# Weight tiles of the second matrix pair used from the buffer in which they are converted, transfers priced by their landing, bucket codes as float32r products

## The chip, the cores and the metric

One core of a Trainium2 chip runs the whole program. The metric is the device time of one execution in microseconds (us); less is better. The core has five engines: TensorE (PE; its weight loads are listed as PEld), VectorE (DVE), ScalarE (ACT), GpSimd (POOL) and SyncE (SP). Each has its own queue of instructions in a fixed order. Sixteen DMA engines move data between DRAM and SBUF. Nearly all transfers are issued from SyncE's queue.

## The reference

The program computes attention in which a query sees the keys of its own hash bucket only, and then two feed-forward blocks.

```python
# q, k, v: (2, 8, 768, 64) float32; proj: (64, 6)
q_bits = (einsum('bhsd,dk->bhsk', q, proj) > 0)
k_bits = (einsum('bhsd,dk->bhsk', k, proj) > 0)
q_bucket = sum(q_bits * 2**arange(6))
k_bucket = sum(k_bits * 2**arange(6))
scores = 0.125 * q @ k.T                       # per head
scores = where(q_bucket == k_bucket, scores, -1e9)
attn = softmax(scores)
x = (attn @ v) -> (1536, 512)
# block 1: w_in (512, 2048), w_out (2048, 512)
x = (s * relu(x @ w_in)**2 + b) @ w_out
# block 2: its own w_in, w_out
h = x @ w_in
out = (h * clip(h + 3, 0, 6) / 6) @ w_out      # (1536, 512)
```

The weight inputs are handed to the kernel as 64-bit words, two 32-bit words for each weight, and the kernel makes float32 of them on the chip.

## The kernel before

**Work.** The 1536 tokens are four units of 384 tokens. Attention runs over 16 pairs (a unit and two heads), and each pair has six slots (one head, 128 queries): 96 slots. A slot is a chain over engines: scores in float32r (`qk`, L417), row maximum (`smax`, L423, VectorE), exponent (`sexp`, L433, ScalarE), six transposes (`turn`, L439), eviction (`evict`, L452 or L454). After six slots come the products with V (`pv_mm`, L494). Before a pair's slots its keys and queries are loaded, split into a high and a low float32r part, and given bucket columns: the product with the projection (`bits_mm`, L379), the comparison with 0 (`bits`, L386), the product with a code matrix of +1 and -1 (`code_mm`, L393), and the comparison with the number of ones (`buckets`). The keys of the first four pairs are stored to DRAM (`k_store`, L327) and fetched again for the next unit (`k_fetch`, L330).

**Jobs.** The feed-forward part is eight jobs (`JOBS`, L30), each one block m for one unit j: (0,0), (0,1), (1,0), (1,1), (0,2), (0,3), (1,2), (1,3). A job goes through 32 weight tiles of 128 x 512: 16 of `w_in`, 16 of `w_out`. Each tile gives 12 matmuls of 128 x 128 by 384 columns (`mm`, L582): high part times high and low input, low part times high input. The numbers in `JOBS` (24, 16, 16, 16, 0 ...) say how many slots of attention of later units are due beside each job.

**Weight tiles.** A raw tile of 512 KB is loaded (`w_load`, L518) into one of three `wr` buffers. `w_exp` (L526, ScalarE) shifts the exponent. `w_ends` extracts two 16-bit halves into a `wf` buffer: the first on any of three engines (L538 on GpSimd, L540 on ScalarE), the second on VectorE (L535). `w_join` (L544, VectorE) joins them to float32. `w_store` (L550) writes the 256 KB to DRAM. For use, a tile is in a `wf` buffer (there are four): `w_hi` (L559, ScalarE) makes the high part in one of three `wh` buffers, `w_lo` (L565, GpSimd) the low part in one of three `wl` buffers. Job 0 uses its tiles from the `wf` buffer in which they were converted ("direct"). Every other job fetches them from DRAM (`w_fetch`, L554). The second pair of matrices is first used in job 2; in the kernel before it is converted ahead of that, stored, and then fetched by job 2 as by any other. Lines 740 to 758 hold this:

```python
direct = m == 0 and i < DIRECT                 # DIRECT = 32, so all of m == 0
ck = key if direct else ("c", m, i)
tw = t - 4.0 if direct else t - 12.0
add("DMA", tw - 4.0, (0.45, 1.46), w_load, (m, i, ck), needs=[("k", 1)] if m == 0 else [("mm", 1, 0)], ...
```

**The order.** Nothing is scheduled by hand: class `Plan` (L35) holds every step with its engine or engines, its duration, its due time, what it needs and gives, and the buffers that it takes and frees. `forward` is a list scheduler with a small model of the engines and of the DMA queue; `backward` turns a plan into latest start times, which are the due times of the next pass. `order` (L72) makes six passes and keeps the plan with the shortest modelled span. The steps are then issued in that order, so each engine's queue has a fixed order, and a step whose buffer or input is late holds all that stands behind it on its engine. A buffer is free when all the steps in its release list are done: a direct tile's `wf` when both the store and `w_lo` are.

**The first stage.** Unit 0's attention runs alone, with more score and raw buffers. Its tiles and buffers then give way to the 16 `G` tiles (the inner activations) and the `X` tiles (`later_units`, L289), which need the PV products and the key stores of the first four pairs.

Of the kernel before, what the change touches and what calls it, by code (L numbers as in the profile page):

```python
# [34 lines left out]
class Plan:  # L35
# [5 lines left out]
    PASSES, PREFER, BOOST = 6, 0, 30  # L41
    SAFE, LAT, DMA_LAT, SAME = 0.5, 0.2, 0.7, {"DVE": 0.1, "ACT": 0.1, "POOL": 0.1}

    WEIGHT = {"DVE": 1.0, "ACT": 0.7}
    EPS = {"PE": 0, "ACT": 0.15, "DVE": 0.3, "POOL": 0.15, "SP": 0.3}
# [26 lines left out]
    def order(self):  # L72

        due, best = [o[1] for o in self.ops], None
        for _ in range(self.PASSES):
            plan = self.forward(due)
            if best is None or plan[0] < best[0]:
                best = plan
            due = [min(x, o[9]) for x, o in zip(self.backward(*plan[:5]), self.ops)]
        self.span, self.log, self.where = best[0], best[5], best[6]  # L80
        return best[4]
# [45 lines left out]
    def forward(self, due):  # L127
# [13 lines left out]
        while left:  # L141
            able = {}
            for o in ready:
# [9 lines left out]
                else:  # L153
                    pick = None
                    for eng, dur in o[0].items():
                        wait = fits
                        for k in o[5]:
                            end, of = self.done[k]
                            wait = max(wait, end + (self.LAT if of != eng else self.SAME.get(eng, 0.0)))
                        if eng == "DMA":  # L160
                            wait = max(wait, clock["HW"], lanes[-8])
                            t, on = max(clock["SP"], wait), "SP"
                            if max(clock["ACT"], wait + self.SAFE) + self.PREFER < t:
                                t, on = max(clock["ACT"], wait + self.SAFE), "ACT"
# [4 lines left out]
                        end += self.WEIGHT.get(eng, 0.0) * (0 if eng == "DMA" else dur)  # L169
                        if pick is None or end < pick[0]:  # L170
                            pick = end, t, on, eng
# [26 lines left out]
            if eng == "DMA":  # L198
                clock["HW"] = t + dur[0]
                start = max(t + dur[0] + self.DMA_LAT, clock["DMA"])  # L200
                clock["DMA"] = end = start + dur[1]
                clock[on] = t + 0.1 if on == "ACT" else t + dur[0]
                lanes.append(end + self.LAT)
                of = "DMA queue"
            elif eng == "PE":
                clock[eng] = end = self.array(t, dur, 0.3 if fn.__name__ == "bits_mm" else 1.0)
                of = eng
            else:
                clock[eng] = end = t + dur
                of = eng  # L210
# [18 lines left out]
def attn_moe_moe2(ctx, tc, qT, kT, vN, cst, w1_in, w1_out, w2_in, w2_out, out):  # L229
# [35 lines left out]

    cv = const.tile([128, 420], F32, name="cv")
# [116 lines left out]
    def bits(g, nm):  # L383
        n = 128 if nm == "k" else 64
        t = at_p.tile([128, 384], F16, tag="bt", name="bt")
        nc.vector.tensor_scalar(out=t[0:n], in0=pd[g][nm + "h"][0:n, 0:384], scalar1=0.0, scalar2=None, op0=ALU.is_gt)  # L386
        pd[g][nm + "b"] = t

    def code_mm(g, nm, h):
        n = 128 if nm == "k" else 64  # L390
# [281 lines left out]
    for g in range(NP):  # L672
        u, hp = pairs[g]
        t = A[SPP * g] - 12.0
        own = new_keys(g)
        old = [g - 1] if 4 < g < 9 else [g - 2, g - 1] if g > 8 else [0] if g == 4 else []
        kfree = [("qk", SPP * x + i) for x in old for i in range(SPP)] + ([("ks", 0, 0), ("ks", 0, 1)] if g == 4 else [])
# [3 lines left out]
        if fetched:  # L681
            for x in range(2):
                add("DMA", t, (0.62, 2.2), k_fetch, (g, x), needs=kfree + [("ks", g - 4, 0), ("ks", g - 4, 1)], gives=[("kh", "kl")[x:x + 1] + (g,)])
        elif own:
            add("DMA", t, (0.62, 2.2), load_k, (g,), acq=[(("kr", "krx") if g < 4 else "kr", ("kr", g))], gives=[("k", g)])
            add({"ACT": 1.5, "POOL": 4.1, "DVE": 1.3}, t, 0, k_hi, (g,), needs=kfree + [("k", g)], gives=[("kh", g)], rel=[(("kr", g), 3)])
            add({"POOL": 3.7, "DVE": 2.0}, t, 0, k_lo, (g,), needs=[("kh", g)], gives=[("kl", g)], rel=[(("kr", g), 3)])
            if g < 4:
                for x in range(2):
                    add("DMA", t + 20.0, (0.62, 2.2), k_store, (g, x), needs=[("kl", g), ("kB", g), ("kB", g, 0)] if x else [("kh", g)], gives=[("ks", g, x)])  # L690
        add("DMA", t, (0.62, 1.1), load_q, (g,), acq=[(("qr", "qrx") if g < 4 else "qr", ("qr", g))], gives=[("q", g)])
        add({"ACT": 0.84, "POOL": 2.6, "DVE": 0.7}, t, 0, q_hi, (g,), needs=qfree + [("q", g)], gives=[("qh", g)], rel=[(("qr", g), 4)])
        add({"ACT": 0.84, "POOL": 2.4, "DVE": 0.7}, t, 0, q_top, (g,), needs=qfree + [("q", g)], gives=[("qt", g)], rel=[(("qr", g), 4)])
        add({"POOL": 4.0, "DVE": 1.22}, t, 0, q_lo, (g,), needs=[("qh", g)], gives=[("ql", g)], rel=[(("qr", g), 4)])
        for nm in ("kq" if own and not fetched else "q"):
            nh = 2 if nm == "k" else 1
            key = ("h", nm, g)
            add("PE", t, 0.85, bits_mm, (g, nm), needs=(kfree if nm == "k" else qfree) + [(nm, g)], acq=[(St, key)],
                gives=[(nm + "m", g)], rel=[((nm + "r", g), 3 if nm == "k" else 4)])
            add("DVE", t, 0.56, bits, (g, nm), needs=[(nm + "m", g)], acq=[("bt", ("bt", nm, g))], gives=[(nm + "b", g)])  # L700
            for h in range(nh):
                last = h == nh - 1
                add("PE", t, 0.5, code_mm, (g, nm, h), needs=[(nm + "b", g)] + ([(nm + "B", g, 0), "cd"] if h else ["cd"]),
                    gives=[(nm + "c", g, h)], rel=[(("bt", nm, g),)] if last else [])
                add({"DVE": 1.02} if nm == "q" else {"ACT": 0.85, "DVE": 1.02}, t, 0, buckets, (g, nm, h), needs=[(nm + "c", g, h)], gives=[(nm + "B", g, h), (nm + "B", g)] if last else [(nm + "B", g, h)],
                    rel=[(key,)] if last else [])
# [27 lines left out]
    for jn, (m, j, n) in enumerate(JOBS):  # L734
        t0, dt = M[jn]
        prev = [("mm", jn - 1, 28 + f // 4) if jn else None for f in range(16)]
        for i in range(32):
            key = (jn, i)
            t = t0 + i * dt
            if jn == first[m]:  # L740
                direct = m == 0 and i < DIRECT
                ck = key if direct else ("c", m, i)
                tw = t - 4.0 if direct else t - 12.0
                add("DMA", tw - 4.0, (0.45, 1.46), w_load, (m, i, ck), needs=[("k", 1)] if m == 0 else [("mm", 1, 0)],
                    acq=[("wr", ("wr", ck))], gives=[("wr",) + ck])
# [5 lines left out]
                last = [(("wf", ck), 1 + direct)]  # L751
                add("DMA", tw, (0.45, 0.73), w_store, (m, i, ck), needs=[("wf",) + ck], gives=[("ws", m, i)], rel=last)
            if jn != first[m] or not direct:
                add("DMA", t - 4.0, (0.45, 0.73), w_fetch, (m, i, key), needs=[("ws", m, i)] + past(jn, i, AHEAD) + before("wi", jn, i),
                    acq=[("wf", ("wf", key))], gives=[("wf",) + key, ("wi",) + key])
# [22 lines left out]
            elif i % 4 == 3:  # L778
# [73 lines left out]
```

## Time and profile before

| | |
|---|---|
| median of 3 runs | 870.61 us (866.76 to 871.86) |
| profiled execution | 870.84 us, its span 868.7 us |
| TensorE busy (PE), weight loads | 819.5 us (94%), 714.3 us (82%) |
| VectorE, ScalarE, GpSimd busy | 453.8, 533.9, 450.0 us |
| mean granted TensorE clock | 0.969 of full |
| DMA moved | 144.72 MB |
| transfers | 64 raw weight loads, 64 stores and 224 fetches of weight tiles |

The page cuts the span in 40 slices and gives every engine's busy share in each. TensorE's slices are at 7 to 9 tenths up to 360 us and at 9 from there, and its clock is at 8 or 9 tenths in the first two slices and between about 220 and 360 us. A busy TensorE is not one at its peak, since its matmuls are pipelined and their ends are modelled; for a stage the count of matmuls beside its length says more than the busy share.

### The profile page before, as it was taken

What the parts mean: (1) busy time and instruction counts of PE and PEld (TensorE: products, weight loads), DVE (VectorE), ACT (ScalarE), POOL (GpSimd) and SP (SyncE); (2) the same over time, 40 slices, a digit from 0 to 9 for tenths busy, and PEclk for the clock granted to TensorE, in tenths of its full rate; (3) what the DMA queues carried; (4) which work ended last, traced back from release to release, by engine and by line L of the source; (5) the groups of instructions that cost most, each with busy time, mean ns of one, the idle gap of its engine ahead of it and who ended that gap; (6) DMA issues with size and microseconds to landing.
All of it is one profiled execution on the core that took longest, in us unless ns stands there. A gap on an engine that the chain in (4) does not pass through costs nothing.

```text
span 868.7 us, 13213 instructions
## 1 busy us (share of the span) xinstructions
PE 819.5 (94%) x4668; PEld 714.3 (82%) x4668; DVE 453.8 (52%) x649; ACT 533.9 (61%) x965; POOL 450.0 (52%) x341
## 2 busy tenths in 40 slices
PE   7898899999887798899999999999999999999998
PEld 2555678879676776888787988889998999999998
DVE  6986489889485657574243656215423511510520
ACT  5766578868465655677474767547564744744742
POOL 4631076778463564653343445336544665665664
PEclk8899999999998879999999999999999999999999
DMA  9954077887577898643433323234433443444442
GB/s 354 396 186 146 19 237 233 226 292 231 175 243 241 283 316 254 215 125 107 119 109 112 103 92 112 88 98 126 118 90 86 123 132 121 125 140 149 124 140 75
DMA packets 63313, 144.72 MB, mean 167 GB/s; under 512 B 6800, under 2 KB 13072, under 8 KB 63248
## 3 DMA queue, kind: packets, MB, share of 16 engines
q1 hardware_dynamic: 63104, 143.68, 51.5%
q8 instruction: 36, 0.59, 0.3%
q14 instruction: 29, 0.24, 0.1%
q10 hardware_dynamic: 144, 0.22, 0.1%
HBM read 117.66 MB, written 26.21 MB: 166 GB/s over the span
## 4 chain that ended last, share of the span: by engine, by line
PE 73%; DMA 11%; DVE 7%; ACT 5%; issue 2%; POOL 1%; SPq 0%; DVEq 0%; ACTq 0%; POOLq 0%
PE mm L582 52%; PE S L417 6%; PE pv L494 6%; PE S L439 6%; DMA w<-wf 3%; DMA wr<-w_out 2%; DMA wr<-w_in 2%; DVE wf L544 2%; DVE wf L535 2%; DMA wf<-w 2%; ACT P L433 1%; PE S L379 1%; DVE nx L423 1%; PE S L393 1%; DVE Q L343 1%
## 5 line engine op out<-in xcount | busy, mean ns | idle before, releaser
L565 POOL TENSOR_TENSOR wl<-wf,wh 128x512 fp32r<-128x512 f32 x256 | 340.0, 1330 | 323.5 <-ACT wh L559 308.6
L582 PE MATMUL mm<-X,wh 128*128 128x384 f32 x1024 | 270.5, 346 | 10.5 <-DVE G L614 10.5
L582 PE MATMUL mm<-G,wh 128*128 128x384 f32 x1024 | 273.5, 349 | 0.7 <-ACT wh L559 0.7
L559 ACT CAST wh<-wf 128x512 fp32r<-128x512 f32 x256 | 157.8, 618 | 119.9 <-PE mm L582 61.8
L582 PEld LDWEIGHTS mm<-X,wh 128*128 128x128 f32 x1024 | 184.4, 191 | 18.6 <-DVE G L614 12.3
L582 PEld LDWEIGHTS mm<-G,wh 128*128 128x128 f32 x1024 | 183.8, 192 | 15.2 <-issue 11.9
L582 PE MATMUL mm<-G,wl 128*128 128x384 f32 x512 | 175.7, 343 | 5.2 <-POOL wl L565 5.2
L582 PE MATMUL mm<-X,wl 128*128 128x384 f32 x512 | 174.4, 341 | 0.3 <-POOL wl L565 0.3
L423 DVE TENSOR_REDUCE nx<-S 128x1 f32<-128x768 f32 x96 | 91.0, 954 | 83.6 <-PE S L417 82.9
L433 ACT ACTIVATE P<-S,nx 128x768 f32<-128x768 f32 x96 | 86.6, 903 | 44.1 <-DVE nx L423 43.7
L582 PEld LDWEIGHTS mm<-G,wl 128*128 128x128 f32 x512 | 98.2, 192 | 6.5 <-POOL wl L565 6.5
L582 PEld LDWEIGHTS mm<-X,wl 128*128 128x128 f32 x512 | 97.9, 191 | 0.6 <-POOL wl L565 0.6
L439 PE MATMUL S<-cv,P 128*128 128x128 f32 x576 | 83.3, 283 | 9.5 <-ACT P L433 9.4
L439 PEld LDWEIGHTS S<-cv,P 128*128 128x128 f32 x576 | 69.2, 145 | 22.6 <-ACT P L433 16.5
L452 ACT COPY pt<-S 128x768 f32<-128x768 f32 x79 | 63.1, 801 | 27.0 <-PE S L439 26.8
L417 PE MATMUL S<-K,Q 128*128 128x512 f32 (+1 forms) x312 | 70.5, 353 | 0.6 <-ACT pt L452 0.5
L526 ACT ACTIVATE wr<-wr 128x512 f32<-128x512 f32 x64 | 43.3, 677 | 41.6 <-DMA wr<-w_out 20.6
L538 POOL TENSOR_SCALAR wf<-wr 128x512 uint16<-128x512 uint16 x53 | 46.9, 886 | 37.8 <-DMA wr<-w_in 14.2
L494 PE MATMUL pv<-pt,v 128*64 128x384 f32 x336 | 63.2, 502 | 0.0
L544 DVE SCALAR_TENSOR_TENSOR wf<-wr,wf 128x512 int32<-128x512 int32 x64 | 56.8, 888 | 7.8 <-POOL wf L538 2.6
L417 PEld LDWEIGHTS S<-K,Q 128*128 128x128 f32 x312 | 53.1, 197 | 8.5 <-issue 2.6
L535 DVE TENSOR_SCALAR wf<-wr 128x512 uint16<-128x512 uint16 x64 | 51.2, 803 | 16.0 <-ACT wr L526 9.2
(359 smaller groups left out, 714.2 us busy)
## 6 DMA issues: line engine op xcount, KB each, us to landing
wf<-w SPq DMA_DIRECT2D x224, 256.0 KB, 2.6
wr<-w_in SPq DMA_DIRECT2D x32, 512.0 KB, 5.0
w<-wf SPq DMA_DIRECT2D x64, 256.0 KB, 4.5
wr<-w_out SPq DMA_DIRECT2D x32, 512.0 KB, 5.1
v<-v_n SPq DMA_DIRECT2D x16, 384.0 KB, 3.8
K<-ks SPq DMA_DIRECT2D x8, 768.0 KB, 6.3
qr<-q_t SPq DMA_DIRECT2D x14, 384.0 KB, 3.9
kr<-k_t SPq DMA_DIRECT2D x6, 768.0 KB, 4.7
```

Source lines behind the costliest of these rows:

```text
L417: nc.tensor.matmul(out=sp[:, c0:c1], lhsT=queries(g)[a][:, h, 128 * t:128 * t + 128], rhs=keys(g)[a][:, h, c0:c1], start=(a == 0), stop=(a ...
L423: nc.vector.reduce_max(out=nx, in_=sd[s]["sp"][:, 0:S], axis=AX.X, negate=True)
L433: nc.scalar.activation(out=d["p"], in_=d["sp"][:, 0:S], func=AF.Exp, bias=d["nx"], scale=1.0, accum_out=pd[g]["sums"][:, c:c + 1])
L439: nc.tensor.transpose(d["sp"][:, 128 * c:128 * c + 128], d["p"][:, 128 * c:128 * c + 128], ident)
L452: nc.scalar.copy(dst, src)
L494: nc.tensor.matmul(out=d["pv"][64 * h:64 * h + 64, 0:NQ], lhsT=d["v"][:, c, 64 * h:64 * h + 64], rhs=d[h][:, c, :], start=(c == 0), stop=( ...
L535: nc.vector.tensor_scalar(out=f16, in0=r16, scalar1=(13, 0x8000)[half], scalar2=None, op0=(ALU.logical_shift_right, ALU.bitwise_and)[half])
L538: nc.gpsimd.tensor_scalar(out=f16, in0=r16, scalar1=2.0 ** -13, scalar2=2.0 ** -14 - 0.5, op0=ALU.mult, op1=ALU.add)
L544: nc.vector.scalar_tensor_tensor(out=wf, in0=wq[key]["raw"][:, :, 1], scalar=3, in1=wf, op0=ALU.logical_shift_left, op1=ALU.bitwise_or)
L559: nc.scalar.copy(hi.rearrange("p a b -> p (a b)"), wq[key]["wf"])
L565: nc.gpsimd.tensor_tensor(out=lo.rearrange("p a b -> p (a b)"), in0=d["wf"], in1=d["hi"].rearrange("p a b -> p (a b)").bitcast(F32), op=AL ...
L582: nc.tensor.matmul(out=a, lhsT=w[:, k, :], rhs=src[k][:, xi, :], start=(k0 + k == 0 and p == 0), stop=(k0 + k == nk - 1 and p == 2))
```

## The change

It has five parts.

1. `direct` is true for both pairs of matrices. The second pair is converted in job 2 itself and used from the buffer of the conversion; the store stays, since jobs 3, 6 and 7 fetch the tiles. The load of tile i of that job may start when the product of the tile eight before is done (`past(jn, i, AHEAD)`), no longer after tile 0 of job 1.
2. The first pair's loads need the PV products of pair 0 (`("pv", 0)`), before they needed the keys of pair 1. Both key stores of a pair need that pair's PV products.
3. All steps that prepare pair 0 get a due time of at most -40.
4. The planner prices a transfer with a third number, the time from its last byte to its landing as consumers see it (`dur[2]`), and `DMA_LAT` goes from 0.7 to 1.4. The key "wi", which only fixes the order in which `wf` buffers are taken, is given at the start of a step. The weights on VectorE's and ScalarE's durations in the choice of an engine are no longer fixed: five sets are tried with six passes each.
5. The bit and code tiles are float32r. A code product takes 32 rows of the code tile and writes all 128 partitions, where it took 64 or 128 rows in float16 and wrote 64 partitions. The constant input shrinks from 420 to 292 columns.

```diff
-    SAFE, LAT, DMA_LAT, SAME = 0.5, 0.2, 0.7, {...}
-    WEIGHT = {"DVE": 1.0, "ACT": 0.7}
+    SAFE, LAT, DMA_LAT, SAME = 0.5, 0.2, 1.4, {...}
+    WEIGHTS = (1.0, 0.7, 0.0), (0.5, 0.5, 0.0), (0.3, 0.0, 0.0), (1.0, 1.0, 0.3), (2.0, 1.0, 0.0)
...
     def order(self):
-        due, best = [o[1] for o in self.ops], None
-        for _ in range(self.PASSES):
-            plan = self.forward(due)
...
+        best = None
+        for dve, act, pool in self.WEIGHTS:
+            self.weight = {"DVE": dve, "ACT": act, "POOL": pool}
+            due = [o[1] for o in self.ops]
+            for _ in range(self.PASSES):
+                plan = self.forward(due)
...
                 clock["DMA"] = end = start + dur[1]
+                end += dur[2]
...
-                self.done[k] = end, of
+                self.done[k] = t - self.LAT if k[0] == "wi" else end, of
...
-    codes = const.tile([128, 4, 64], F16, name="codes")
+    codes = const.tile([128, 128], F32R, name="codes")
...
-        t = at_p.tile([128, 384], F16, tag="bt", name="bt")
+        t = at_p.tile([128, 384], F32R, tag="bt", name="bt")
...
     def code_mm(g, nm, h):
         for i in range(2):
-            nc.tensor.matmul(out=t[64:128, 512 * i:512 * i + 384], lhsT=codes[0:n, 2 * h + i, :], rhs=bt[0:n],
-                             start=True, stop=True)
+            r = slice(64 * h + 32 * i, 64 * h + 32 * i + 32)
+            nc.tensor.matmul(out=t[:, 512 * i:512 * i + 384], lhsT=codes[r], rhs=bt[r], start=True, stop=True)
...
+        first_of_all = -40.0 if g == 0 else 1e9
...
-                    add("DMA", t + 20.0, (0.62, 2.2), k_store, (g, x), needs=[("kl", g), ("kB", g), ("kB", g, 0)] if x else [("kh", g)], ...
+                    add("DMA", t + 20.0, (0.62, 2.2, 1.5), k_store, (g, x), needs=[("kl", g), ("kB", g), ("kB", g, 0), ("pv", g)], ...
...
-                direct = m == 0 and i < DIRECT
+                direct = True
...
-                add("DMA", tw - 4.0, (0.45, 1.46), w_load, (m, i, ck), needs=[("k", 1)] if m == 0 else [("mm", 1, 0)],
+                add("DMA", tw - 4.0, (0.45, 1.46, 0.8), w_load, (m, i, ck), needs=[("pv", 0)] if m == 0 else past(jn, i, AHEAD) if direct else [("mm", 1, 0)],
...
-                add("DMA", tw, (0.45, 0.73), w_store, (m, i, ck), needs=[("wf",) + ck], gives=[("ws", m, i)], rel=last)
+                add("DMA", tw, (0.45, 0.73, 1.9), w_store, (m, i, ck), needs=[("wf",) + ck], gives=[("ws", m, i)], rel=last)
```

The other transfers get their third number in the same way (loads of keys 0.3, of queries and V 0.8, key fetches 1.0, weight fetches 0.0, output stores 1.5).

## Rows read from the trace of the kernel before

**Rows 1.** Windows by stage: stretch, its length, engines' busy us and counts, clock, DMA.
```profile
core 0: us, PE busy (x) PEld busy (x) DVE busy (x) ACT busy (x) POOL busy (x), PEclk, DMA share, GB/s
0.00:18.00 18.00, 11.92 (x48) 3.53 (x48) 10.52 (x11) 10.31 (x11) 9.24 (x8) 0.87 0.92 342
18.00:60.00 42.00, 37.79 (x212) 24.13 (x212) 40.52 (x49) 30.70 (x52) 22.38 (x14) 0.89 0.80 309
60.00:101.00 41.00, 34.40 (x203) 21.45 (x200) 24.03 (x36) 24.47 (x44) 2.42 (x1) 1.00 0.32 107
101.00:231.00 130.00, 125.70 (x747) 104.34 (x746) 103.97 (x138) 93.59 (x173) 88.17 (x63) 0.99 0.68 220
231.00:357.00 126.00, 103.55 (x510) 92.99 (x509) 83.20 (x119) 74.11 (x135) 68.77 (x59) 0.86 0.79 267
357.00:471.00 114.00, 111.80 (x659) 94.01 (x658) 52.22 (x74) 73.29 (x131) 50.15 (x36) 0.99 0.40 121
471.00:582.00 111.00, 111.00 (x670) 95.58 (x670) 49.60 (x76) 70.60 (x129) 46.44 (x35) 1.00 0.32 99
```
**Rows 2.** The same windows for the weight products of line L582 alone (PE, PEld).
```profile
664.00:731.00 67.00, 67.00 (x385) 67.00 (x385) 1.00 0.44 126
```
**Rows 3.** The same windows for the score products of line L417, four to a slot.
```profile
18.00:60.00 42.00, 13.32 (x52) 9.26 (x52) 0.89 0.80 309
60.00:101.00 41.00, 13.23 (x56) 8.46 (x56) 1.00 0.32 107
101.00:231.00 130.00, 18.20 (x84) 13.42 (x84) 0.99 0.68 220
231.00:357.00 126.00, 9.40 (x40) 7.57 (x40) 0.86 0.79 267
357.00:471.00 114.00, 12.97 (x60) 9.99 (x60) 0.99 0.40 121
471.00:582.00 111.00, 14.78 (x68) 11.27 (x68) 1.00 0.32 99
```
**Rows 4.** Chain of waits within 231:357, shares by engine and line.
```profile
by line: DMA w<-wf 20.7%; DMA wr<-w_in 12.6%; DMA wf<-w 10.7%; DVE wf L535 8.9%; issue 8.2%; DMA wr<-w_out 7.8%; DVE wf L544 7.2%; ACT wr L526 4.7%; PE mm L582 3.9%; POOL wl L565 2.5%; ACT wh L559 2.3%; ACT G L606 2.0%; SPq L550 1.5%; ACT w
```
**Rows 5.** SyncE's queue waits, total us, times, longest: first 101:231, then 231:357.
```profile
SPq L518 <- DVE wf L544: 51.7, 20, 5.5
...
SPq L554 <- DMA w<-wf: 35.9, 15, 5.0
```
**Rows 6.** Groups by line within 101:231: busy us, mean ns | idle before.
```profile
L544 DVE SCALAR_TENSOR_TENSOR wf<-wr,wf 128x512 int32<-128x512 int32 x25 | 24.2, 966 | 1.0
L535 DVE TENSOR_SCALAR wf<-wr 128x512 uint16<-128x512 uint16 x25 | 22.4, 896 | 3.5 <-ACT wr L526 3.4
```
**Rows 7.** SyncE's timeline, 0:48: start us, us, instruction.
```profile
7.14 0.33 SPq L327 DMA_DIRECT2D ks<-K  x1
7.51 1.52 SPq L518 DMA_DIRECT2D wr<-w_in  x3
...
10.67 0.33 SPq L317 DMA_DIRECT2D kr<-k_t  x1
```
**Rows 8.** Page, DMA issues: count, KB each, median us from issue to landing.
```profile
wf<-w SPq DMA_DIRECT2D x224, 256.0 KB, 2.6
wr<-w_in SPq DMA_DIRECT2D x32, 512.0 KB, 5.0
w<-wf SPq DMA_DIRECT2D x64, 256.0 KB, 4.5
...
ks<-K SPq DMA_DIRECT2D x2, 768.0 KB, 8.0
```
**Rows 9.** The windows of Rows 1 for the joins of line L544 alone (DVE).
```profile
18.00:60.00 42.00, 4.36 (x5) 0.89 0.80 309
```
**Rows 10.** Chain of waits within 101:231 in order of time: start us, us, what.
```profile
106.59 0.77 PE S L379 x4
...
108.68 0.44 PE S L393 x2
```

More of the change, by code (lines that the diff above doesn't have):

```diff
@@ L168, in forward @@
                             end = t + dur
-                        end += self.WEIGHT.get(eng, 0.0) * (0 if eng == "DMA" else dur)
+                        end += 0 if eng == "DMA" else self.weight.get(eng, 0.0) * dur
                         if pick is None or end < pick[0]:
@@ L682, in attn_moe_moe2 @@
             for x in range(2):
-                add("DMA", t, (0.62, 2.2), k_fetch, (g, x), needs=kfree + [("ks", g - 4, 0), ("ks", g - 4, 1)], gives=[("kh", "kl")[x:x + 1] + (g,)])
+                add("DMA", t, (0.62, 2.2, 1.0), k_fetch, (g, x), needs=kfree + [("ks", g - 4, 0), ("ks", g - 4, 1)], gives=[("kh", "kl")[x:x + 1] + (g,)])
         elif own:
-            add("DMA", t, (0.62, 2.2), load_k, (g,), acq=[(("kr", "krx") if g < 4 else "kr", ("kr", g))], gives=[("k", g)])
-            add({"ACT": 1.5, "POOL": 4.1, "DVE": 1.3}, t, 0, k_hi, (g,), needs=kfree + [("k", g)], gives=[("kh", g)], rel=[(("kr", g), 3)])
@@ L687, in attn_moe_moe2 @@
-            add({"POOL": 3.7, "DVE": 2.0}, t, 0, k_lo, (g,), needs=[("kh", g)], gives=[("kl", g)], rel=[(("kr", g), 3)])
+            add("DMA", t, (0.62, 2.2, 0.3), load_k, (g,), acq=[(("kr", "krx") if g < 4 else "kr", ("kr", g))], gives=[("k", g)], soon=first_of_all)
+            add({"ACT": 1.5, "POOL": 4.1, "DVE": 1.3}, t, 0, k_hi, (g,), needs=kfree + [("k", g)], gives=[("kh", g)], rel=[(("kr", g), 3)], soon=first_of_all)
+            add({"POOL": 3.7, "DVE": 2.0}, t, 0, k_lo, (g,), needs=[("kh", g)], gives=[("kl", g)], rel=[(("kr", g), 3)], soon=first_of_all)
@@ L688, in attn_moe_moe2 @@
             if g < 4:
                 for x in range(2):
[L690 to L693, printed above, removed]
@@ L694, in attn_moe_moe2 @@
-        add({"POOL": 4.0, "DVE": 1.22}, t, 0, q_lo, (g,), needs=[("qh", g)], gives=[("ql", g)], rel=[(("qr", g), 4)])
+                    add("DMA", t + 20.0, (0.62, 2.2, 1.5), k_store, (g, x), needs=[("kl", g), ("kB", g), ("kB", g, 0), ("pv", g)], gives=[("ks", g, x)])
+        add("DMA", t, (0.62, 1.1, 0.8), load_q, (g,), acq=[(("qr", "qrx") if g < 4 else "qr", ("qr", g))], gives=[("q", g)], soon=first_of_all)
+        add({"ACT": 0.84, "POOL": 2.6, "DVE": 0.7}, t, 0, q_hi, (g,), needs=qfree + [("q", g)], gives=[("qh", g)], rel=[(("qr", g), 4)], soon=first_of_all)
@@ L784, in attn_moe_moe2 @@
                     add("ACT", te, 0.48, o_copy, (j, d, key), needs=[("mm", jn, i)], acq=[("o", ("o", key))], gives=[("o", jn, d)], rel=[(acc_key,)])
-                    add("DMA", te, (0.45, 0.55), o_store, (j, d, key), needs=[("o", jn, d)], gives=[("os", jn, d)], rel=[(("o", key),)])
-    add("DVE", 0.0, 0.2, lambda: nc.vector.tensor_copy(out=codes.rearrange("p a b -> p (a b)"), in_=cv[:, 164:420]), (), gives=["cd"])
+                    add("DMA", te, (0.45, 0.55, 1.5), o_store, (j, d, key), needs=[("o", jn, d)], gives=[("os", jn, d)], rel=[(("o", key),)])
+    add("DVE", 0.0, 0.2, lambda: nc.vector.tensor_copy(out=codes, in_=cv[:, 164:292]), (), gives=["cd"])
     with tc.manual_schedule():
@@ L827 @@
     bucket = np.arange(64)
-    cst = np.zeros((128, 420), np.float32)
+    cst = np.zeros((128, 292), np.float32)
     for c in range(NB):
```

29 lines of the change are left out of this document (15 added, 14 removed).

## The prediction

> **What bounds the kernel now.** I read the windows by stage first, because the page's 94% of busy TensorE mixes stages with different limits. The 3072 weight products come in eight jobs of 384, so the count of products cuts the span into jobs: the stretch 664:731 holds one job and nothing else, 67.0 us for 385 products, 0.174 us each [rows 2]. The score products (four to a slot) tell how many slots of attention each job carries [rows 3]: 27 slots before the first job, then 21, 10, 15 and 17. Job 3 (471:582) has TensorE busy throughout: 111 - 67 = 44 us for 17 slots, 2.59 us a slot. With these two prices each job has a floor, and what lies above is loss:
> - job 0 (101:231): 130 - 67 - 21 x 2.59 = 8.6 us
> - job 1 (231:357): 126 - 67 - 10 x 2.59 = 33.1 us
> - job 2 (357:471): 114 - 67 - 15 x 2.59 = 8.2 us
> - job 3: none, by construction of the price.
>
> So the reader is to see one sick stage. In job 1 TensorE is busy 103.6 of 126 us, at a granted clock of 0.86 of full, part of it at the 1.2 GHz level, and the DMA engines at 0.79; all other jobs have 0.99 or 1.00 of clock [rows 1]. The chain of that stretch names the cause: a fifth of it is landings of converted tiles' stores, then weight loads, fetches and conversion steps; products are 3.9% [rows 4]. Job 1 converts all 32 tiles of the second matrix pair for job 2 beside its own work. Both use the same four buffers "wf", so SyncE's queue stands with a fetch at its head waiting for a store to land, 35.9 us in 15 waits [rows 5].
>
> The second place is the first stage: 101 us for 27 slots, whose TensorE work is 27 x 2.59 = 70 us. From 18 to 60 VectorE is busy 40.5 of 42 us, and the DMA engines stand at 0.92 and 0.80 until 60, then at 0.32 [rows 1].
>
> **The change part by part.** Sums are made against the profiled execution, 870.84 us (span 868.7 and 2.1 around it); the median of the runs is 870.61, so no correction.
>
> 1. *Second pair converted in its own job.* Job 1 loses 32 conversions with their loads and stores; job 2 gets them and loses 32 fetches. The code has no other user of "wf" in job 1 than the fetches then, which is what job 3 does at no loss and job 2 at 8.2. I take 4 us of loss left, 29 gained; bounds 25 (job 2's loss) and 33 (none).
> What job 2 gets: VectorE does 52.2 us there now [rows 1]; a tile adds a half-word step of 0.896 and a join of 0.966 us, as measured in job 0, which converts and uses tiles in place [rows 6]: 32 x 1.862 = 59.6, together 111.8 us. TensorE's floor there is 105.8 us. Seven tiles (four wf and three wh buffers) can be converted before job 2 begins, 13.0 us, which leaves 98.8. Job 0 sustained VectorE at 104.0 of 130 us, 0.80 [rows 1]; at that share 98.8 us take 123.5, and without any head start 111.8 take 139.8. The lower end is the floor, 105.8; job 0's loss on it gives 114.4. I take 121, near the VectorE end because that is the nearest row: +7 against today's 114, bounds -8 and +26. The buffers allow it: a tile keeps its wf for 1.9 us of VectorE work, a first half-word of about the same 0.9, and the store's 4.5 us landing [rows 8], 7.3 us over four buffers, 1.8 us a tile against 3.8 us of pace. The store's landing is then beside the product's own preparation, so it is hidden as long as loads come early; the price if they don't is the last rival.
>
> 2. *Weight loads only after the first pair's PV, key stores only after their pair's PV, first pair's steps urgent.* Now three weight loads (1.5 MB) and a key store stand in SyncE's queue at 7.1 to 9 us, ahead of the next pair's keys at 10.7 [rows 7]; five joins lie in the full VectorE stretch, 4.4 us, and with the half-words (0.896 each) 8.8 us [rows 6, 9]. They go to 60:101, where VectorE has 17 us idle and the DMA engines two thirds. What is late next there is the slot chain itself (scores, maximum, exponent, transposes), and some of the moved work will stand in its way. I take 6 us gained; bounds 0 (all comes back after 60) and 13 (101 us less 70 of TensorE work and the 18 before the first scores).
>
> 3. *The G buffers.* They lie over the first unit's tiles and need the last key stores landed; these now start only with pair 3's PV, and the slowest of them took 8.0 us [rows 8]. Three accumulators and the slots of the next pair cover most of it; behind a late G waits ScalarE's queue, and with it the next weight's high part. +1, bounds 0 and 8.
>
> 4. *Bucket codes.* A pair of code products takes 0.44 us in the chain [rows 10]. In the new form (32 rows, full width) the nearest rows are two ordinary products, 0.35 [rows 2], and four narrow products in 0.77 [rows 10]. There are 32 pairs, so -3 to +11 if all lay on the path; the chosen price is 0, since two of a narrow form lie between both rows. The smaller constant and bit tiles add no instruction.
>
> 5. *The order is written anew.* Transfers are priced with their landing, and five weightings are tried. Where the order now issues a load too late it shows in job 0, whose loss is 8.6 us. I take 2 of it as gained; bounds 8.6 (all) and -6.4 (it rises to the 15 that I give job 2).
>
> Sum: 870.84 - 29 + 7 - 6 + 1 + 0 - 2 = **842 us**.
>
> **The rivals.**
> - *VectorE bounds job 2.* No head start, so 139.8 us instead of 121: 842 + 19 = 861. For it: VectorE's demand would exceed TensorE's floor there. Against: slots can move to job 1, which has only 10, and each takes about (104.0 - 25 x 1.862)/21 = 2.7 us of VectorE with it (the job's own evictions included).
> - *More than I give.* First stage at its floor (-13, not -6) and job 0 without loss (-8.6, not -2): 842 - 7 - 6.6 = 828. For it: the DMA queue is full exactly where the inputs are late [rows 1, 7]. Against: the tiles still have to be converted before job 0 starts.
> - *It comes back elsewhere.* VectorE-bound job 2, and nothing in the first stage: 861 + 6 = 867, within 0.5%, which is about what a measurement can tell from no change.
> - *Slower: job 2 runs at the pace of a load that is issued too late.* Today a tile passes through DRAM and may be converted a job ahead; then a product waits directly on load, conversion and buffer. The place is SyncE's queue: a store waits at its head for a join (51.7 us in 20 waits in job 0, 2.6 each [rows 5]) and the next load stands behind it. If the wf buffers are full too, a raw buffer is held for load 5.0, queue 2.6, conversion 1.9 + 0.9, and another store's landing 4.5 [rows 6, 8]: 14.9 us over three buffers is 5.0 us a tile, 159 us for the job, 38 more than my 121: 880. It decides against the change from job 2 at about 154 us on. For it: job 1 now goes at 3.9 us a tile in this way with a clock that falls. Against: job 0 has the same path with more slots and goes at 4.1 with 8.6 us of loss.
> The Trainium skill has a rule that speaks for this rival: in "DMA: Bandwidth & Descriptors", section "Anatomy of one DMA", it says that a transfer's semaphore fires only when the last byte is confirmed at the target, and that this is slowest towards HBM. The trace agrees: 4.5 us for a store and 2.6 for a fetch of the same 256 KB [rows 8]. By the rule the wait stands however the queue is arranged, and the sum would be this rival's 880; by the rows of job 0 it lies beside the products, and the sum is 842.
>
> **How the numbers follow.** Forecast 0.62 (own range 831 to 853), VectorE-bound 0.17, more than I give 0.10, comes back 0.04, slower 0.07. The range 822 to 864 leaves out the last two, the upper part of the VectorE case and the low tail, about 0.2. Faster by over 0.5%: 0.62 + 0.17 + 0.10 = 0.89; same 0.04; slower 0.07.
>
> **What would show it.** Step 1: job 1 at about 97 us for 10 slots (or 2.59 more for each further slot), clock near 1.0, no weight loads in it but the last few tiles'; 192 fetches instead of 224; job 2 at 115 to 124 with VectorE near 0.8. Step 2: no weight load before 40 us, first stage at about 95 us. Step 3: first write of G within 3 us of what the products allow. Step 4: a code pair still between 0.35 and 0.77 us. I am wrong in the main step if job 1 keeps over 15 us of loss, and in its price if job 2 takes over 130 us.

## The result and the profile after

The changed kernel takes 829.39 us (median of 4 runs, 824.88 to 830.71) beside 868.68 us of the kernel before: a ratio of 0.9535 (of the means), 95% interval 0.9485 to 0.9586. The forecast was 842, with 822 to 864 as its range. The profiled execution took 830.71 us, its span 828.8.

The windows by stage of the changed kernel, cut where its jobs begin (columns as in [rows 1]; each of the four stretches from 104 on holds 383 to 386 weight products):

```profile
0.00:18.00 18.00, 8.70 (x34) 2.69 (x34) 11.48 (x9) 9.98 (x11) 7.03 (x6) 0.78 0.70 250
18.00:60.00 42.00, 37.57 (x208) 24.30 (x210) 25.92 (x32) 29.52 (x48) 11.92 (x7) 0.85 0.50 178
60.00:104.00 44.00, 37.60 (x218) 24.24 (x215) 29.45 (x44) 31.35 (x58) 10.04 (x9) 0.92 0.75 260
104.00:232.00 128.00, 124.22 (x751) 103.88 (x750) 98.80 (x137) 92.48 (x174) 93.00 (x64) 1.00 0.67 218
232.00:304.00 72.00, 72.00 (x415) 70.73 (x415) 31.12 (x48) 45.56 (x84) 46.60 (x38) 1.00 0.55 165
304.00:422.00 118.00, 115.85 (x696) 98.63 (x695) 92.89 (x130) 93.37 (x171) 84.66 (x65) 1.00 0.72 226
422.00:542.00 120.00, 120.00 (x727) 100.03 (x726) 56.12 (x81) 79.79 (x144) 58.47 (x40) 1.00 0.34 102
```

The same windows for the score products (line L421 now), four to a slot, which answer to [rows 3]:

```profile
18.00:60.00 42.00, 15.25 (x56) 10.85 (x56) 0.85 0.50 178
60.00:104.00 44.00, 12.51 (x48) 8.20 (x48) 0.92 0.75 260
104.00:232.00 128.00, 18.51 (x88) 14.30 (x88) 1.00 0.67 218
232.00:304.00 72.00, 3.27 (x16) 2.63 (x16) 1.00 0.55 165
304.00:422.00 118.00, 17.56 (x80) 12.82 (x80) 1.00 0.72 226
422.00:542.00 120.00, 15.55 (x73) 11.89 (x72) 1.00 0.34 102
```

The reader is to see where the 40 us went. Jobs 1 to 3 together took 351 us with 42 slots [rows 1, 3]; they now take 310 us with 42 slots, 41 less. At 67 us a job and 2.59 a slot, 41.2 us of loss became 0.2. Job 0 went from 130 us with 21 slots to 128 with 22. The first stage got longer: 104 us with 26 slots, where it was 101 with 27. What lies behind 542 is unchanged. A single job's loss can come out below zero now, because a slot is counted where its scores stand and its transposes and PV products may fall into the next job; the three jobs are best read together.

The chain of waits within job 1 of the changed kernel, which answers to [rows 4]:

```profile
by line: PE mm L586 93.3%; PE S L421 3.9%; PE S L443 1.8%; PE S L398 1.0%
```

Landings of stores, weight loads and conversion steps are gone from it, and products went from 3.9% to 93.3%. SyncE's queue in that job (total us, times, longest), which answers to the second line of [rows 5], has its fetches wait for the last user of a buffer and for no store:

```profile
SPq L558 <- POOL wl L569: 43.9, 27, 2.1
SPq L522 <- DVE wf L548: 14.4, 4, 4.6
```

Job 2 now has the conversions. Its queue still shows what the slower rival was about, a load behind a store that waits for a join, and the groups of the two VectorE steps of a conversion there answer to [rows 6]:

```profile
SPq L522 <- DVE wf L548: 46.1, 20, 5.0
```

```profile
L548 DVE SCALAR_TENSOR_TENSOR wf<-wr,wf 128x512 int32<-128x512 int32 x29 | 30.6, 1056 | 1.0
L539 DVE TENSOR_SCALAR wf<-wr 128x512 uint16<-128x512 uint16 x28 | 20.8, 744 | 2.7 <-ACT wr L530 2.3 <-issue 0.4
```

A join and a half-word step together take 1.80 us, where 1.86 were reckoned with. The page's transfers, which answer to [rows 8], show 32 fetches fewer and the same landings of fetches and stores:

```profile
wf<-w SPq DMA_DIRECT2D x192, 256.0 KB, 2.6
wr<-w_in SPq DMA_DIRECT2D x32, 512.0 KB, 4.3
w<-wf SPq DMA_DIRECT2D x64, 256.0 KB, 4.5
```

### The profile page after: what moved, and what is told of

It reads as the page before. It is cut to its first block, busy times and chain, and to the rows that moved or that the text cites. A ratio compares the mean times of both kernels' runs of the same rounds, so it can differ in the third digit from the quotient of the medians.

```text
span 828.8 us, 13143 instructions
## 1 busy us (share of the span) xinstructions
PE 799.3 (96%) x4668; PEld 702.9 (85%) x4668; DVE 435.0 (52%) x627; ACT 538.8 (65%) x976; POOL 475.0 (57%) x355
## 4 chain that ended last, share of the span: by engine, by line
PE 86%; DVE 5%; ACT 4%; issue 2%; DMA 1%; POOL 1%; DVEq 0%; ACTq 0%; POOLq 0%
PE mm L586 62%; PE pv L498 7%; PE S L421 7%; PE S L443 7%; ACT P L437 2%; PE S L384 2%; PE S L398 1%; DVE nx L427 1%; DVE wf L548 1%; DMA qr<-q_t 1%; ACT pt L456 1%; DMA wr<-w_out 1%; PE pv L376 1%; DVE Q L370 1%; DVE wf L539 1%
## 5 line engine op out<-in xcount | busy, mean ns | idle before, releaser
L586 PE MATMUL mm<-G,wh 128*128 128x384 f32 x1024 | 267.9, 342 | 0.8 <-DVE G L618 0.8
L586 PE MATMUL mm<-X,wh 128*128 128x384 f32 x1024 | 266.9, 341 | 1.1 <-DVE G L621 0.6
L586 PEld LDWEIGHTS mm<-X,wh 128*128 128x128 f32 x1024 | 181.2, 188 | 11.1 <-issue 4.1
L586 PEld LDWEIGHTS mm<-G,wh 128*128 128x128 f32 x1024 | 180.3, 188 | 9.8 <-issue 6.8
L586 PE MATMUL mm<-G,wl 128*128 128x384 f32 x512 | 172.4, 337 | 0.2 <-POOL wl L569 0.2
L456 ACT COPY pt<-S 128x768 f32<-128x768 f32 x84 | 67.2, 803 | 19.8 <-PE S L443 19.2
L421 PE MATMUL S<-K,Q 128*128 128x512 f32 (+1 forms) x312 | 71.3, 359 | 1.5 <-ACT pt L456 1.2
L548 DVE SCALAR_TENSOR_TENSOR wf<-wr,wf 128x512 int32<-128x512 int32 x64 | 66.1, 1033 | 2.8 <-POOL wf L542 0.7
L421 PEld LDWEIGHTS S<-K,Q 128*128 128x128 f32 x312 | 53.8, 201 | 11.2 <-issue 2.6
L618 DVE SCALAR_TENSOR_TENSOR G<-mm,cv,G 128x384 fp32r<-128x384 f32 x64 | 39.3, 615 | 32.2 <-ACT G L610 32.0
L539 DVE TENSOR_SCALAR wf<-wr 128x512 uint16<-128x512 uint16 x64 | 42.5, 664 | 16.2 <-ACT wr L530 7.3
```

Source lines behind the costliest of these rows:

```text
L421: nc.tensor.matmul(out=sp[:, c0:c1], lhsT=queries(g)[a][:, h, 128 * t:128 * t + 128], rhs=keys(g)[a][:, h, c0:c1], start=(a == 0), stop=(a ...
L456: nc.scalar.copy(dst, src)
L539: nc.vector.tensor_scalar(out=f16, in0=r16, scalar1=(13, 0x8000)[half], scalar2=None, op0=(ALU.logical_shift_right, ALU.bitwise_and)[half])
L548: nc.vector.scalar_tensor_tensor(out=wf, in0=wq[key]["raw"][:, :, 1], scalar=3, in1=wf, op0=ALU.logical_shift_left, op1=ALU.bitwise_or)
L586: nc.tensor.matmul(out=a, lhsT=w[:, k, :], rhs=src[k][:, xi, :], start=(k0 + k == 0 and p == 0), stop=(k0 + k == nk - 1 and p == 2))
```

## The experiments

Each was timed against the kernel before in the same runs. For the table, each trace was cut at its own first products: a job's loss is its length less 67.2 us (the two jobs without slots take 67.1) and 2.59 us a slot; the first stage's excess is the time to the first weight product less 2.59 us for each slot begun until then.

| kernel | median us | ratio, 95% interval | first stage: products at, slots, excess | loss job 0 | loss jobs 1 to 3 | joins in job 1 |
|---|---|---|---|---|---|---|
| before | 868.7 to 871.0 | 1 | 101.3, 27, 31.4 | 8.5 | 40.6 | 32 |
| changed | 829.4 | 0.9535, 0.9485 to 0.9586 | 104.2, 26, 36.9 | 3.4 | 0.4 | 4 |
| direct_only | 833.0 | 0.9577, 0.9541 to 0.9614 | 103.1, 27, 33.2 | 8.5 | 0.7 | 5 |
| all_but_direct | 837.1 | 0.9623, 0.9584 to 0.9662 | 99.5, 27, 29.6 | 1.3 | 14.6 | 21 |
| old_prices | 838.9 | 0.9644, 0.9606 to 0.9682 | 106.0, 26, 38.7 | 3.0 | 9.1 | 5 |
| landing_only | 852.7 | 0.9794, 0.9755 to 0.9833 | 100.3, 27, 30.4 | 2.2 | 28.7 | 24 |
| old_first | 822.5 | 0.9457, 0.9411 to 0.9503 | 96.3, 28, 23.8 | 3.9 | 4.3 | 5 |
| stores_early | 827.5 | 0.9509, 0.9490 to 0.9527 | 97.5, 26, 30.1 | 0.3 | 6.9 | 5 |
| due_old | 826.4 | 0.9495, 0.9478 to 0.9512 | 99.4, 27, 29.4 | 4.1 | 1.8 | 4 |
| loads_early | 820.4 | 0.9428, 0.9404 to 0.9453 | 99.5, 27, 29.5 | 0.8 | 0.2 | 4 |
| klo_on_dve | 824.1 | 0.9482, 0.9449 to 0.9515 | 97.6, 26, 30.3 | 3.3 | 0.0 | 4 |
| warm_early | 829.0 | 0.9523, 0.9481 to 0.9566 | 101.5, 26, 34.2 | 3.3 | 0.4 | 4 |
| f16_codes | 830.0 | 0.9528, 0.9498 to 0.9558 | 102.6, 26, 35.3 | 5.4 | 0.8 | 4 |
| loads_early_klo | 827.7 | 0.9499, 0.9462 to 0.9536 | 99.0, 27, 29.1 | -1.1 | 9.8 | 4 |

One warning stands ahead of all of them. Most edits let the planner write a new order, which changes every stage and not only the edited one. klo_on_dve, warm_early and f16_codes keep the changed kernel's order, and in them jobs 1 to 3 stay at a loss of 0.0 to 0.8 us; only they tell of one cause alone by their time.

**direct_only** has the second pair used in place and nothing else:

```diff
-direct = m == 0 and i < DIRECT
+direct = True
-needs=[("k", 1)] if m == 0 else [("mm", 1, 0)]
+needs=[("k", 1)] if m == 0 else past(jn, i, AHEAD) if direct else [("mm", 1, 0)]
```

> The kernel before with one edit: the second pair of matrices is converted in job 2 and used in place (loads allowed eight tiles ahead); old prices, old first stage, old code products. Theory 1 (job 1 was slow because 32 conversions shared four wf buffers with its fetches, so taking them out is the gain whatever the prices): 828 to 840 us, job 1 with a loss under 5 us over its floor and a granted clock near 1.0. Rival (the new prices make the gain, in place use alone only moves the stall into job 2): over 850 us, job 2 above 130 us with a clock below 0.95.

833.0 us, 0.7 us of loss in jobs 1 to 3. Its windows for jobs 1 and 2:

```profile
233.00:316.00 83.00, 83.00 (x489) 78.05 (x488) 39.28 (x60) 54.61 (x100) 45.59 (x37) 1.00 0.47 150
316.00:427.00 111.00, 107.70 (x640) 92.64 (x639) 98.06 (x125) 90.63 (x167) 84.97 (x62) 1.00 0.71 228
```

Job 1 is busy throughout at full clock, and job 2 does not take the stall over. In-place use is enough by itself for jobs 1 to 3, under the old prices too; job 0 keeps its 8.5 us.

**all_but_direct** undoes only that in the changed kernel.

```diff
-direct = True
+direct = m == 0 and i < DIRECT
```

> The changed kernel with the second pair converted ahead in job 1 and fetched in job 2, as before; new prices, weightings, first stage and code products stay. Theory 1: 858 to 870 us, job 1 again with 25 to 35 us of loss and a clock under 0.92. Rival (prices make the gain): under 845 us, job 1 at a full clock.

It took 837.1 us, far below what my theory gave. The rival's time fits and its full clock nearly (0.98), but jobs 1 to 3 keep 14.6 us of loss: most of the gain is there without in-place use. So in-place use is enough but not needed. Its windows for jobs 1 and 2, and SyncE's waits in job 1:

```profile
222.00:324.00 102.00, 95.69 (x550) 85.07 (x548) 73.11 (x106) 72.59 (x135) 48.65 (x39) 0.98 0.77 265
324.00:427.00 103.00, 98.44 (x578) 87.83 (x578) 59.98 (x87) 71.31 (x131) 54.04 (x39) 0.98 0.59 191
```

```profile
SPq L554 <- DVE wf L548: 20.7, 11, 6.4
SPq L558 <- POOL wl L569: 13.3, 11, 2.9
...
SPq L558 <- DMA w<-wf: 8.8, 6, 2.2
```

The new order converts 21 tiles in job 1 and 11 in job 2, where the old one put all 32 into job 1, and the fetches' wait for a store's landing is 8.8 us in 6 waits instead of 35.9 in 15 [rows 5]. So the stall was not the conversions' mere presence in job 1. That fetches issued behind stores were the whole of it is not shown, as landing_only tells next.

**old_prices** and **landing_only** part the planner's two edits. The first has in-place use with the old prices and weighting, the second the new prices (with the early "wi" and the new code products) and nothing else.

```diff
# old_prices
-SAFE, LAT, DMA_LAT = 0.5, 0.2, 1.4
+SAFE, LAT, DMA_LAT = 0.5, 0.2, 0.7
-                end += dur[2]
-                self.done[k] = t - self.LAT if k[0] == "wi" else end, of
+                self.done[k] = end, of
-    WEIGHTS = (1.0, 0.7, 0.0), (0.5, 0.5, 0.0), (0.3, 0.0, 0.0), (1.0, 1.0, 0.3), (2.0, 1.0, 0.0)
+    WEIGHTS = (1.0, 0.7, 0.0),
# landing_only: direct and WEIGHTS as before, the edits of old_first (below), new prices kept
```

> The changed kernel with the old prices of transfers (no landing time, 0.7 for the start) and the one old weighting; in place use, first stage and code products stay. Theory 1: within 8 us of the changed kernel's 829, since the stall was in buffers and not in the order; job 0's loss goes from 3.6 back towards the 8.6 us of before. Rival: over 845 us.

> In place use, the search over weightings and the first stage's rules are all undone; of the changed kernel only the prices of transfers by landing (and the code products) stay. Theory (the prices alone spread the conversions of the second pair over jobs 1 and 2 and so take most of job 1's stall): 832 to 845 us, fewer than 25 joins in job 1. Rival (the search over weightings found the better order): over 855 us, 32 joins in job 1 and a clock under 0.92 there.

old_prices took 838.9 us, 9.5 more than the changed kernel; that is outside the 8 that I gave, and its job 0 did not go back (3.0). Its jobs 1 to 3 lose 9.1 us, where direct_only, with the same prices and weighting, loses 0.7, so the prices alone do not explain them. landing_only took 852.7: the prices take jobs 1 to 3 from 40.6 to 28.7 us of loss and job 0 from 8.5 to 2.2. Its joins in job 1 are 24 as expected, its time is between both theories. Its job 1 (the second row is job 2):

```profile
224.00:331.00 107.00, 93.29 (x529) 84.34 (x528) 75.96 (x109) 71.30 (x134) 61.18 (x51) 0.98 0.81 264
331.00:445.00 114.00, 106.71 (x612) 92.94 (x611) 65.20 (x87) 72.67 (x129) 58.91 (x42) 0.96 0.53 167
```

Its SyncE waits in job 1, for a store's landing:

```profile
SPq L558 <- DMA w<-wf: 11.9, 8, 3.7
```

That wait fell from 35.9 us to 11.9, and yet 28.7 us of loss stay; on the chain of its job 1 the landings of fetches are 27.4%, those of stores 5.7%. Here a plan that knows the landings took away only part of the stall. Between landing_only and all_but_direct lie the search over weightings and the first stage's rules, 14.1 us in jobs 1 to 3. Which of the two, or merely another order, these runs do not part.

**old_first, stores_early, loads_early, due_old** undo the three rules of the first stage together and one by one.

```diff
# loads_early
-needs=[("pv", 0)] if m == 0 else past(jn, i, AHEAD) ...
+needs=[("k", 1)] if m == 0 else past(jn, i, AHEAD) ...
# stores_early
-needs=[("kl", g), ("kB", g), ("kB", g, 0), ("pv", g)]
+needs=[("kl", g), ("kB", g), ("kB", g, 0)] if x else [("kh", g)]
# due_old
-first_of_all = -40.0 if g == 0 else 1e9
+first_of_all = 1e9
# old_first: all three
```

> The changed kernel with the first stage's rules of before: first weight loads after the keys of pair 1, key stores as soon as each part is ready, no early due time for pair 0. Theory 1 (the rules gained nothing there: VectorE was not what paced 18:60, and loads and stores now crowd 80:90, where a query load takes 6.1 us): 824 to 830 us, job 0 begins at 98 to 102 us instead of 104. Rival (the rules did help, and the slow start is a clash on VectorE that the old rules had worse): 831 to 838 us, job 0 begins after 106 us.

> The changed kernel with one rule of its first stage undone: key stores as soon as each part is ready, not after the pair's PV products. Theory (the late stores crowd the DMA engines at 80:95, where a query load takes 6.1 us and VectorE stands behind it): 822 to 826 us, most of the 7 us that undoing all three rules gave; first products by 100 us. Rival (the start is what costs, the early due time and a clash of VectorE with GpSimd at 8 to 24 us): 828 to 832 us.

> The changed kernel with one rule undone: the first pair's weight loads may start after the keys of pair 1, not after the PV products of pair 0. Theory (what I forecast as a gain, 8.8 us less of VectorE work in 18:60, was none, because VectorE did not pace that stretch; and the tiles converted later crowd 60:104): 824 to 829 us, no slower than the changed kernel although its weight loads start early. Rival (my forecast): 834 to 838 us.

> The changed kernel with one rule undone: no early due time for the steps of pair 0. Theory (stores and loads are the cost): 828 to 832 us, no gain. Rival (the start costs): 820 to 825 us, first scores by 18 us instead of 20.1 and the granted clock over 0.9 between 18 and 60.

All four are faster than the changed kernel by their medians (820.4 to 827.5), and each has 6.8 us or more less excess in the first stage. My ranges mostly missed: old_first and loads_early lie below both of theirs, stores_early and due_old between theory and rival. The excess singles out no rule, and due_old, which was to show nothing, shows as much. The times at which slots begin tell more. The first two rows are the kernel before, the next two the changed one (score products up to 76 us, and from there to the first weight product); the last is the longest wait on the changed kernel's chain of the first stage:

```profile
0.00:76.00 76.00, 19.80 (x80) 13.50 (x80) 0.91 0.81 302
76.00:101.00 25.00, 6.75 (x28) 4.23 (x28) 1.00 0.07 22
0.00:76.00 76.00, 21.00 (x80) 14.47 (x80) 0.87 0.55 197
76.00:104.00 28.00, 6.76 (x24) 4.57 (x24) 0.88 0.87 300
81.08 6.12 DMA qr<-q_t
```

Both kernels have begun 20 slots by 76 us. From there the kernel before needs 25 us for 7 more, with the DMA engines at 0.07, and the changed one 28 us for 6, with the DMA engines at 0.87 and a query load of 6.12 us on its chain. The same split runs through all fourteen kernels: from the 20th slot's first score product to the 27th's, the seven with both late loads and late stores (changed, all_but_direct, old_prices, due_old, klo_on_dve, warm_early, f16_codes) take 28.6 to 31.6 us, and the seven without one or both (before, direct_only, landing_only, old_first, stores_early, loads_early, loads_early_klo) 19.8 to 27.3. So the moved loads and stores do cost time, late in the stage. The early due time is another matter: due_old begins its 20th slot at 67.5 us instead of 74.5, and its next seven still take 31.1. Each of these runs has a new order too, so the size of each rule stays open. loads_early is the best kernel of this study, 0.9428 (0.9404 to 0.9453), below the changed kernel's interval.

**klo_on_dve** keeps the order and moves one kind of step. The changed kernel's VectorE timeline between 7 and 24 us (start us, us, instruction) shows the query low parts, then GpSimd's shows the key low parts:

```profile
8.00 3.53 DVE L370 SCALAR_TENSOR_TENSOR Q<-qr,Q 64x768 fp32r<-64x768 f32 x1
...
12.14 4.22 DVE L370 SCALAR_TENSOR_TENSOR Q<-qrx,Q 64x768 fp32r<-64x768 f32 x1
...
19.72 4.11 DVE L370 SCALAR_TENSOR_TENSOR Q0x<-qr,Q0x 64x768 fp32r<-64x768 f32 x1
```

```profile
7.27 3.43 POOL L355 TENSOR_TENSOR K<-kr,K 64x1536 fp32r<-64x1536 f32 x1 [6.85 <-ACT K L345]
12.13 3.41 POOL L355 TENSOR_TENSOR K1x<-krx,K0x 64x1536 fp32r<-64x1536 f32 x1 [1.43 <-ACT K0x L345]
19.51 3.51 POOL L355 TENSOR_TENSOR K1x<-kr,K0x 64x1536 fp32r<-64x1536 f32 x1 [3.96 <-ACT K0x L345]
```

Each VectorE step ends 0.8 us after the GpSimd step beside it; alone it takes 0.95 us. TensorE meanwhile has nothing to do from 12.9 to 18.0, and its granted clock between 10 and 18 us is 0.50, the 1.2 GHz level.

```diff
+first = next(x for x in steps if x[0] is k_lo and x[1] == (0,))
+steps.remove(first)        # and inserted again just ahead of pair 0's buckets of queries
-for fn, a, on in plan.order():
+for fn, a, on in steps:
+    on = "DVE" if fn is k_lo and a[0] < 4 else on
```

> The changed kernel with its own order of steps kept, but the low part of the first four pairs' keys made on VectorE instead of GpSimd, the first one behind both query low parts. Theory (three low parts of queries take 3.5 to 4.2 us instead of 0.95 because they stand while GpSimd makes a key low part of 3.4 us): these three come to about 0.95 us, first scores at 14 to 16 us instead of 20.1, clock in 18:60 above 0.85, and 824 to 828 us. Rival (the VectorE steps are slow for another reason, or something else ends last there): they stay over 3 us, or the time stays within 2 us of 829.

The same stretch of VectorE's timeline:

```profile
8.01 0.96 DVE L370 SCALAR_TENSOR_TENSOR Q<-qr,Q 64x768 fp32r<-64x768 f32 x1 [0.20 <-ACT Q L345]
...
9.58 0.95 DVE L370 SCALAR_TENSOR_TENSOR Q<-qrx,Q 64x768 fp32r<-64x768 f32 x1
10.56 1.75 DVE L355 TENSOR_TENSOR K<-kr,K 64x1536 fp32r<-64x1536 f32 x1
...
16.70 0.95 DVE L370 SCALAR_TENSOR_TENSOR Q0x<-qr,Q0x 64x768 fp32r<-64x768 f32 x1
```

All three are at 0.95 us, the key low part itself takes 1.75 us here and 3.4 on GpSimd, the first scores stand at 16.1 us instead of 20.1, and the clock in 18:60 is 0.94. The first products come 6.6 us earlier at the same slots, and the span is 7.2 us shorter. By medians it is 824.1 against 829.4 us; the two intervals against the kernel before overlap a little, so the timeline is the proof of the mechanism and the 5 us are its likely size.

**warm_early** keeps the order too and fills TensorE's gaps in the first 18 us.

```diff
+n = {("k", 0): 12, ("q", 0): 22}.get(a[1:], 0) if fn is code_mm and a[0] == 0 else 0
+if n:
+    warm(n)                # 128x512 float16 matmuls on an idle tile
```

> The changed kernel in its own order, with 34 matmuls on an idle tile added where TensorE stands in the first 18 us (12 behind the first code pair, 22 behind the query's). Theory (the granted clock of 0.50 to 0.80 between 10 and 40 us makes the first slots late): clock in 18:60 from 0.85 to over 0.95, 824 to 828 us. Rival (those slots wait for VectorE and ScalarE, and the clock costs nothing): the clock rises and the time stays at 828 to 832.

829.0 us: the rival's time. The two rows are 10:18 and 18:60 of this kernel:

```profile
10.00:18.00 8.00, 7.58 (x37) 3.17 (x34) 7.68 (x5) 2.08 (x3) 4.01 (x2) 1.00 0.57 191
18.00:60.00 42.00, 35.44 (x214) 22.93 (x215) 27.22 (x34) 32.39 (x52) 11.89 (x7) 0.92 0.50 178
```

The clock is full in 10:18 and 0.92 after, and the median is the same within 0.4 us; the profiled span is 2.8 us shorter (826.0 against 828.8). So the slow clock between 10 and 18 us was mainly a sign of the wait, and what it cost by itself is at most about these 3 us. (The clock after 18 us did not reach the 0.95 that I wrote. One of the three long VectorE steps described above moved to another step there, so the run is no clean measure to the microsecond.)

**f16_codes** puts the old code products into the changed kernel's order.

```diff
-codes = const.tile([128, 128], F32R)        # and bit tiles in F32R
+codes = const.tile([128, 4, 64], F16)       # and bit tiles in F16
-nc.tensor.matmul(out=t[:, 512 * i:512 * i + 384], lhsT=codes[r], rhs=bt[r], ...)
+nc.tensor.matmul(out=t[64:128, 512 * i:512 * i + 384], lhsT=codes[0:n, 2 * h + i, :], rhs=bt[0:n], ...)
```

> The changed kernel in its own order of steps, with the old code products (float16 tiles, 64 or 128 rows, 64 columns of weights). Theory (the new form is worth nothing, as I priced it): within 2 us of the changed kernel's 829. Rival (the new form saves 0.1 to 0.2 us in each of 32 pairs): 831 to 836 us.

830.0 us, 0.6 more than the changed kernel, the intervals nearly the same. A pair in the chain of job 0 takes 0.44 us in the old form (first) and 0.38 in the new (second):

```profile
124.03 0.44 PE S L398 x2
```

```profile
125.57 0.38 PE S L398 x2
```

**loads_early_klo** was to add the two gains: loads_early's rule, and the key low parts of the first four pairs planned on VectorE alone.

```diff
-needs=[("pv", 0)] if m == 0 else past(jn, i, AHEAD) ...
+needs=[("k", 1)] if m == 0 else past(jn, i, AHEAD) ...
-add({"POOL": 3.7, "DVE": 2.0}, t, 0, k_lo, ...)
+add({"DVE": 1.8} if g < 4 else {"POOL": 3.7, "DVE": 2.0}, t, 0, k_lo, ...)
```

> A version meant to beat both: the changed kernel with the first pair's weight loads after the keys of pair 1 again, and the key low parts of the first four pairs planned on VectorE alone. If the two gains (9 and 5 us) are different ones they add up: 812 to 818 us. If both are the same early slots: 818 to 822 us.

827.7 us, outside both ranges and worse than loads_early alone. Its first stage is no better (excess 29.1 against 29.5), so the two gains did not add in this order; whether they are the same one stays open. The rest is a new order whose jobs 1 to 3 lose 9.8 us instead of 0.2.

## Why the prediction was right, and where it was not

The time lay in the range and the sign and the place of the gain were right. It lay just below the range of the forecast's own case (831 to 853) and beside the 828 of the rival that gave more, whose mechanism did not happen: the first stage did not reach its floor. By steps, the sum of 842 missed the profiled 830.7 by 11 us, made of errors that partly cancel: jobs 1 to 3 gave 19 us more than forecast and job 0 some 2.6, the first stage took 11.6 more, and the 1 us for the G buffers was not seen. That the sum came so near is in part luck.

*Step 1, second pair in its own job: right in place, too small by 19 us.* I gave 29 gained in job 1 and 7 lost in job 2, net 22; jobs 1 to 3 gave 41. The term that was mis-sized is job 2's. I read VectorE's share of job 0, 0.80, as what VectorE can sustain and let 98.8 us of its work stretch to 121. Job 2 has 92.9 us of it in 118, a share of 0.79, and yet TensorE is the bound, with 20 slots and next to no loss. A share that one stage reached is not a ceiling for another. Nor need all of it be work: in the kernel before a join takes 0.69 us by its median and a half-word step 0.55, but up to 2.58 and 1.67, and the means of 0.966 and 0.896 that I summed hold such long ones. I also had the slots move the wrong way: they went out of job 1 (4 instead of 10) into jobs 2 and 3. The VectorE rival did not happen, nor the slower one, though SyncE's waits of a load behind a store's join are there (46.1 us in 20 waits): job 2 has next to no loss beside them. The rule of the Trainium skill that I quoted ("DMA: Bandwidth & Descriptors", "Anatomy of one DMA") agrees with the 4.5 us of a store again (that section describes transfers that GpSimd issues, these are SyncE's), but in-place use has the landing beside the product's own work.

My reading of the cause was incomplete. I took the conversions in job 1 for the fault; all_but_direct shows that most of the loss (40.6 us to 14.6) goes with the conversions still partly there, once the order is written anew with prices by landing, a search over weightings and the first stage's rules; the prices without the other two leave 28.7. Each side does most of the work without the other, and their gains do not add: 833.0 us with in-place use only, 837.1 with everything else, 829.4 with both.

*Step 2, the first stage: failed.* I forecast 6 us gained from 8.8 us less of VectorE work in 18:60. That work did leave: VectorE went from 40.5 to 25.9 us of 42, and the slots begun there from 13 to 14 [rows 1, 3]. A full VectorE was not what paced the slots. The stage lost 3 us and a slot, some 5.6 us at 2.59 a slot, and it lost them after 76 us, until where both kernels had begun 20 slots: there the moved loads and stores stand beside the next query load. I had named that ("some of the moved work will stand in its way") and given 0 as the worst case; the bound was wrong.

klo_on_dve shows a second loss: three query low parts that stood for 3.4 us of GpSimd each. Without them the 20th slot begins 5.4 us earlier, at 69.1 us, and the next seven still take 29.1. The kernel before had such waits as well (4.07 and 3.10 us for a query low part), so they do not make the difference between the two kernels, and the excess of 30.3 us without them is no fair match for its 31.4. The early due time gained nothing either, by due_old. The rules together were no gain here; how much each costs stays open.

*Step 3, the G buffers: priced at 1, nothing seen.* The first write of G starts at 111.3 us, 2 us after the first tile's last product, within the 3 that I named.

*Step 4, code products: right.* A pair fell between my two rows (0.35 and 0.77) at 0.38 us, and f16_codes is the same in time.

*Step 5, the new order: right in sign, too small in job 0 and misplaced.* Job 0 gained about 5 us instead of 2. The runs don't single out its cause: landing_only has it (2.2 us of loss) and old_prices too (3.0); direct_only alone stays at 8.5. What I did not see is that a new order mends job 1 as well, so that it is a second cause of the main gain.

## What to carry to other kernels

Read a stall by what stands at the head of the queue: here a fetch that waited for a store to land. Taking the store out of the way mended it. An order that knows when a store lands mended a part, with a search over weightings and other rules most of it, and these gains don't add. A full engine is a bound only if the work behind it is late: take some of it away in thought and ask what comes next; VectorE lost 14.6 us of work in a 42 us stretch and bought one slot. Follow the work that you move to where it lands: here it met a query load at 81 us. When an order is written by a planner, an edit of one rule is tested only with the rest of the order held; loads_early and loads_early_klo differ by 9.6 us in jobs 1 to 3, where nothing was edited.

## What the runs showed of the hardware that was not expected

A VectorE instruction with two inputs in SBUF stood still while a GpSimd instruction of two inputs ran: the query low part of 0.95 us took 3.53, 4.22 and 4.11 us beside key low parts of 3.4 to 3.5 us, and 0.95 each time once GpSimd was idle. The Trainium skill says so in "SBUF — State Buffer", section "Who interferes with whom": VectorE and GpSimd share a port pair that is an exclusive lock, and a VectorE instruction with two inputs in SBUF contends with a GpSimd instruction that reads SBUF. The trace agrees: each step ends 0.8 us after GpSimd's, about what it takes alone. Two more rows bear on it. Beside a GpSimd instruction of one input (`TENSOR_SCALAR`) the query low part took 1.46 us (at 87.8 us in the changed kernel), though that instruction ran 2.5 us. In warm_early a VectorE instruction with one input (L348, 0.55 us otherwise) took 3.61 us beside a key low part. The planner prices the two steps as independent, 1.22 and 3.7 us, so its order puts them side by side. The kernel before paid for it as well: its query low part at 11.1 us took 4.07.
